# Strassen's method, one level, for the channel-mixing output product of batches 1 to 7

## The chip, the cores and the metric

The kernel runs on one core of one Trainium2 chip. The metric is the device time of one execution in microseconds (us). Before the change three runs gave 285.89, 285.95 and 286.25; their median, 285.95 us, is the time before. The engines are called PE (the matrix engine, TensorE), DVE (VectorE), ACT (ScalarE), POOL (GpSimd) and SP (SyncE, which here issues nearly all transfers).

## The reference

Attention over 8 batches, 8 heads, 576 positions and head dimension 64, with a plain window of 32 in heads 0 to 3 and a dilated one (every fourth position, reach 128) in heads 4 to 7, and a mixer behind it:

```python
attn = softmax(mask(q @ k.T / sqrt(D)))        # per batch and head
x    = (attn @ v) as [B, S, H * D]             # 8 x 576 x 512
h    = relu(x.T @ w_tok1) @ w_tok2             # token mixing, 576 -> 256 -> 576
u    = x + h.T
h2   = relu(u @ w_ch1) @ w_ch2                 # channel mixing, 512 -> 1536 -> 512
out  = u + h2
```

The change is in the last product, `relu(u @ w_ch1) @ w_ch2`, of 512 of the 576 positions of a batch (the last 64, the tail, are done for two batches together), and in the sum with u.

## The kernel before, in words

All operands of products are fp16, sums are fp32 in PSUM. A matmul takes a 128x128 block that stands still (lhsT) and streams up to 512 columns past it.

**One batch in the main line (`gen_main`, L747).** First the hidden layer: for each of 12 blocks `mb` of 128 hidden channels, four matmuls of 512 columns (L768, `gp`) and a ReLU into `gt` (L771; on ACT, of some blocks on DVE). In odd batches the tail of two batches comes in between (L759, `gt<-utt`). `gt` holds, for each hidden block, the columns of an even batch (0 to 511), of the tail (512 to 639) and of an odd batch (640 to 1151). Then the output product: for each of four row tiles `s` and each half of 256 output columns, 12 matmuls of 256 columns (L801, `yp`), so 96 per batch; in odd batches also 12 of 512 columns for the tail (L818), ahead of them. DVE adds u (L809) out of PSUM into `o32`, and SP stores two halves (L814). In the last batch the last row tile is cut into three narrower pieces (L787 to L795).

**Row order.** u's first two blocks of channels (plain heads) lie in natural row order. The other two (dilated heads) lie in the order of residue modulo 4: tile `s` holds rows s, s+4, s+8 and so on. That is why the second half of a row tile reads `gt` with a step of 4 (`a0:m0 + 512:4`, L804) and is stored with a stride. The hidden layer needs u with channels in the partitions: a DMA transpose (`uT_dma`, L682) turns all of u into `utm`, and ACT copies its dilated blocks into natural order into `utd` (`uT_place`, L690). Batch 0 and 1 do this on PE (`emit_uT`, L656).

**What is fed into the main line.** Each batch has a list of steps with a due time and a cost in us, written by hand (L1017 to L1064): values of the next batch (`values`, L592, heads 0 to 7), its token mixing (`emit_h1`, `emit_u` L630, `uT_dma`, `uT_place`), casts (L274), DMA transposes (`dma_steps`, L348) and placements (`place_steps`, L393) of q and k of the batch after next, its scores (`scores_twin`, L498), and loads three batches ahead. `interleave` (L827) advances a clock by the costs that the main line yields and emits a step when its due time has come. Each engine and each queue then works in the order of emission.

**Scores.** `scores_twin` runs for batches 2 to 7 in two groups, g = 0 (plain heads) and g = 1 (dilated heads): matmuls into six PSUM banks, exponentials on ACT (L534), and masks by multiplication on POOL (L112, `attp`, `attd`, `attt`).

**PSUM.** Eight banks: three called `main` in rotation (hidden layer, output product, one bank of scores), three `fl` (values, token mixing, u, scores), two `sc` (scores).

Of the kernel before, what the change touches and what calls it, by code (L numbers as in the profile page):

```python
# [9 lines left out]
FP16 = mybir.dt.float16  # L10
# [4 lines left out]
B = 8  # L15
# [53 lines left out]
def kernel(  # L69
# [19 lines left out]
    turn = {"main": 0, "sc": 0}  # L89

    def bank(tag, bufs, name, dtype=FP32):

        if tag in turn:
# [37 lines left out]
    qza = fixed("qz", [128, 4, 2, S])  # L131
    qz = [qza[:, i] for i in range(4)]
# [155 lines left out]
    xn, u16w, uT = {}, {}, {}  # L288
# [209 lines left out]
    def scores_twin(b, g):  # L498
# [72 lines left out]

        yield from small_exps(1)
        if b == 2:
            yield from small_exps(0)
        for hp in (2 * g, 2 * g + 1):
            for h in range(2):
                main(hp, h)
                if h and (g or b == 2):
                    mask(hp)
                    if b == 2 and hp % 2 == 0:  # L580
                        mask_tails()
                yield 0.0
        if b > 2:
            yield from small_exps(0)
            if g == 0:
                mask(0)
            mask_tails()
            if g == 0:
                mask(1)
# [66 lines left out]
    def emit_uT(b, cb):  # L656
        odd = b % 2
        p = bank("fl" if b or cb % 2 == 0 else "main", 3, f"tpu_{b}_{cb}", FP16)
        t = sb.tile([128, 640 if odd else 512], FP16, tag=f"ut{odd}", bufs=4, name=f"uT_{b}_{cb}")
# [22 lines left out]
    def uT_dma(b, tail):  # L682
# [3 lines left out]
        else:  # L686
            nc.sync.dma_start_transpose(out=uTm[i].rearrange("p x s t -> p (x s) t"),
                                        in_=u16w[b].rearrange("p x s c -> p (x s c)"))

# [57 lines left out]
    def gen_main(b):  # L747
# [28 lines left out]
        last = b == B - 1  # L776
        for s in ((4, 0, 1, 2, 3) if odd else (0, 1, 2, 3)):
            p = bank("main", 3, f"yp_{b}_{s}")
            o32 = sb.tile([128, DM], FP32, tag="o32", bufs=4, name=f"o32_{b}_{s}")
            if last and s == 3:  # L780
                for c0, n in ((0, 256), (256, 128), (384, 128)):
                    c = slice(c0, c0 + n)
                    if c0:
                        p = bank("main", 3, f"yq_{b}_{c0}")
                    a0 = m0 + (s if c0 else 128 * s)
                    for mb in range(NMB):
                        nc.tensor.matmul(  # L787
                            out=p[:, c], lhsT=gta[:, mb, a0:m0 + 512:4] if c0 else gta[:, mb, a0:a0 + 128],
                            rhs=w4[mb][:, c], start=(mb == 0), stop=(mb == NMB - 1))
                    nc.vector.tensor_tensor(out=blocks4(o32[:, c]), in0=blocks4(p[:, c]),  # L790
                                            in1=u16(b, s)[:, c0 // 128:(c0 + n) // 128], op=ALU.add)
                    nc.sync.dma_start(
                        out=out[b, 0:512, c].rearrange("(m r) c -> r m c", r=4)[s] if c0 else
                        out[b, 128 * s:128 * s + 128, c], in_=o32[:, c])
                    yield 0.65  # L795
            elif s < 4:
                for half in range(2):
                    c = slice(256 * half, 256 * half + 256)
                    for mb in range(NMB):
                        a0 = m0 + (s if half else 128 * s)  # L800
                        nc.tensor.matmul(  # L801
                            out=p[:, c],
                            lhsT=gta[:, mb, a0:m0 + 512:4] if half else
                            gta[:, mb, a0:a0 + 128],  # L804
                            rhs=w4[mb][:, c], start=(mb == 0), stop=(mb == NMB - 1))
                        if mb == 5:
                            yield 0.65
                    if half:
                        nc.vector.tensor_tensor(out=blocks4(o32), in0=blocks4(p), in1=u16(b, s), op=ALU.add)  # L809
                        for i in range(2):  # L810
                            d = slice(256 * i, 256 * i + 256)
# [283 lines left out]
```

## Time and profile before

| | |
|---|---|
| median of three runs | 285.95 us |
| the profiled execution's span | 284.4 us |
| PE busy | 276.2 us (97%) |
| DVE, ACT, POOL busy | 130.7, 136.9, 163.3 us |
| output product (L801), 744 matmuls of 256 columns | 85.8 us busy, mean 273 ns |
| hidden layer (L768), 144 + 144 + 96 matmuls of 512 columns | 54.7 + 54.6 + 25.8 us busy |
| DMA engines, mean busy share by the queues' packets | q1 69.2%, q0 7.9% |

How to read the profile: every line of a group gives source line, engine, operation, output <- input, shape and count, then busy time and the mean of one instruction in ns, then the idle time of the engine before these instructions and what ended it. In a timeline a row begins with the start and the length in us; several like instructions in a row are merged (x24), and idle time before a row stands in brackets with what ended it. Matmuls are pipelined: the next begins before the last has ended, so a matmul's own length says little of its pace. The profiled execution is one run; its span runs from the first to the last instruction.

### The profile page before, as it was taken

The page shows a single profiled execution, that of the slowest core. Times are in us where ns is not written, and L with a number is a line of the kernel's source. Part 1 is how long each engine was busy: PE and PEld are TensorE (multiplying, and loading weights), DVE is VectorE, ACT ScalarE, POOL GpSimd, SP SyncE. Part 2 cuts the span into 40 slices and gives each one's busy share as a digit, 9 for nine tenths or more (in the row PEclk, how much of TensorE's full clock was granted, in tenths as well). Part 3 has the DMA queues.
Part 4 walks back from the last instruction along what each step waited for, and adds up shares of the span by engine and source line. Part 5 has one row for each costly group of instructions (what it writes and reads, how often), then busy time and mean ns, then how long its engine had stood idle before and what let it go on. Part 6 is the DMA issues. An engine that isn't in the chain of part 4 may idle for free.

```text
span 284.4 us, 7021 instructions
## 1 busy us (share of the span) xinstructions
PE 276.2 (97%) x2850; PEld 210.9 (74%) x2850; DVE 130.7 (46%) x275; ACT 136.9 (48%) x270; POOL 163.3 (57%) x220
## 2 busy tenths in 40 slices
PE   6899999999999999999999999999999999999995
PEld 2786677887676976697776976797767966896595
DVE  7776676356764155415640254426441274421022
ACT  2863765454454615383446625482546534225500
POOL 7980760587936998459961999179953930000000
PEclk9999999999999999999999999999999999999999
DMA  7999999984999999999979988299974210431023
GB/s 218 265 227 253 271 218 211 323 206 117 342 187 142 292 275 236 145 223 334 195 151 227 312 239 169 58 236 313 203 146 85 94 56 2 92 112 39 0 76 111
DMA packets 105695, 52.63 MB, mean 185 GB/s; under 512 B 73888, under 2 KB 104608, under 8 KB 105664
## 3 DMA queue, kind: packets, MB, share of 16 engines
q1 hardware_dynamic: 101424, 47.07, 69.2%
q0 software_dynamic: 2640, 3.94, 7.9%
q10 hardware_dynamic: 1600, 1.18, 1.4%
q8 instruction: 22, 0.36, 0.6%
q14 instruction: 9, 0.07, 0.1%
HBM read 37.07 MB, written 9.44 MB: 163 GB/s over the span
## 4 chain that ended last, share of the span: by engine, by line
PE 79%; DMA 7%; POOL 6%; SPq 2%; DVE 2%; issue 1%; ACT 1%; POOLq 0%; ACTq 0%
PE gp L768 25%; PE yp L801 25%; PE h1p L627 4%; PE gt L759 4%; PE up L639 4%; PE yp L818 3%; PE sc L510 2%; DMA l_k<-in_k_dram 2%; DMA w1p<-in_moe_w_tok_dram 2%; DMA kr<-c_k 2%; DMA l_q<-in_q_dram 2%; POOL c_q L102 1%; PE av L603 1%; PE av L608 1%; PE h1p L625 1%
## 5 line engine op out<-in xcount | busy, mean ns | idle before, releaser
L801 PE MATMUL yp<-w,gt 128*128 128x256 f16 x744 | 85.8, 273 | 0.0
L801 PEld LDWEIGHTS <-gt 128*128 128x128 f16 x744 | 76.1, 106 | 6.4
L106 ACT ACTIVATE gt<-gp 128x512 f16<-128x512 f32 x71 | 42.4, 597 | 73.5 <-PE gp L768 73.2
L768 PE MATMUL gp<-utd,w 128*128 128x512 f16 x144 | 54.7, 380 | 0.0
L768 PE MATMUL gp<-utm,w 128*128 128x512 f16 x144 | 54.6, 379 | 0.0
L768 PEld LDWEIGHTS <-w 128*128 128x128 f16 x384 | 38.9, 114 | 19.7 <-issue 0.5
L809 DVE TENSOR_TENSOR o<-yp,u 128x512 f32<-128x512 f32 x31 | 21.4, 692 | 63.4 <-PE yp L801 63.4
L112 POOL TENSOR_TENSOR attp<-attp,const 128x1280 f16<-128x1280 f16 x12 | 31.4, 2616 | 24.4 <-ACT attp L534 24.3
L112 DVE TENSOR_TENSOR xn<-av,rec 128x320 f16<-128x320 f32 x64 | 31.5, 492 | 2.2
L112 POOL TENSOR_TENSOR attd<-attd,const 128x1024 f16<-128x1024 f16 x12 | 25.4, 2134 | 1.9 <-ACT attd L534 1.9
L768 PE MATMUL gp<-uT,w 128*128 128x512 f16 x96 | 25.8, 380 | 0.0
L108 DVE TENSOR_SCALAR gt<-gp 128x512 f16<-128x512 f32 x25 | 17.2, 688 | 13.7 <-PE gp L768 13.0
L645 DVE TENSOR_TENSOR u<-up,xn 128x512 f16<-128x512 f32 x26 | 17.9, 690 | 6.2 <-PE up L639 6.2
L534 ACT ACTIVATE attp<-sc 128x480 f16<-128x480 f32 (+1 forms) x36 | 16.1, 536 | 7.3 <-PE sc L510 6.2
L102 POOL CAST c_k<-l_k 128x512 f16<-128x512 f32 x29 | 17.7, 622 | 2.1 <-DMA l_k<-in_k_dram 2.0
L102 POOL CAST c_q<-l_q 128x512 f16<-128x512 f32 x26 | 16.7, 648 | 2.5 <-DMA l_q<-in_q_dram 1.8
L106 ACT ACTIVATE h<-h1p 128x256 f16<-128x256 f32 x31 | 11.9, 384 | 11.9 <-PE h1p L627 11.5
L616 DVE RECIPROCAL rec<-av 128x5 f32<-128x5 f32 x64 | 12.2, 191 | 9.8 <-PE av L613 9.6
L399 POOL COPY kt<-kr 128x512 f16<-128x512 f16 x10 | 10.8, 1078 | 9.9 <-DMA kr<-c_k 7.7
L697 ACT COPY utd<-utm 128x512 f16<-128x512 f16 x12 | 12.7, 1117 | 5.8 <-DMA utm<-u 5.8
L102 POOL CAST vv<-l_vn 128x256 f16<-128x256 f32 x32 | 11.9, 413 | 4.0 <-DMA l_vn<-in_v_dram 4.0
L112 POOL TENSOR_TENSOR attt<-attt,const 128x512 f16<-128x512 f16 x12 | 13.9, 1162 | 0.0
(149 smaller groups left out, 465.2 us busy)
## 6 DMA issues: line engine op xcount, KB each, us to landing
out_dram<-o SPq DMA_DIRECT2D x71, 128.0 KB, 3.2
l_q<-in_q_dram SPq DMA_DIRECT2D x15, 512.0 KB, 6.7
l_k<-in_k_dram SPq DMA_DIRECT2D x14, 512.0 KB, 7.1
l_vn<-in_v_dram SPq DMA_DIRECT2D x32, 128.0 KB, 6.4
l_vd<-in_v_dram SPq DMA_DIRECT2D x16, 256.0 KB, 4.5
w<-in_moe_w_ch_dram POOLq DMA_DIRECT2D x6, 512.0 KB, 7.6
lt<-in_q_dram SPq DMA_DIRECT2D x8, 128.0 KB, 3.9
l_vt<-in_v_dram SPq DMA_DIRECT2D x8, 128.0 KB, 4.1
```

The lines of the kernel that those rows point to most:

```text
L102: eng.tensor_copy(out=out, in_=in_)
L106: nc.scalar.activation(out=out, in_=in_, func=AF.Relu)
L108: eng.tensor_scalar_max(out=out, in0=in_, scalar1=0.0)
L112: eng.tensor_tensor(out=out, in0=x, in1=y, op=ALU.mult)
L534: nc.scalar.activation(out=out, in_=in_, func=AF.Exp, scale=0.125)
L616: nc.vector.reciprocal(out=rec[:, :, 0], in_=av[:, :, 64])
L627: nc.tensor.matmul(out=p, lhsT=w[:, s, j], rhs=x[:, s, c], start=False, stop=(s == 3))
L645: nc.vector.tensor_tensor(out=u16(b, s), in0=blocks4(p), in1=blocks4(xn[b][:, s]), op=ALU.add)
L697: nc.scalar.copy(out=natural(uTd[:, cb - 2]), in_=uTm[i][:, cb].rearrange("p r m -> p m r"))
L768: nc.tensor.matmul(out=p, lhsT=w3_block(cb, mb), rhs=uT[(b, cb)][0], start=(i == 0), stop=(i == 3))
L801: nc.tensor.matmul(out=p[:, c], lhsT=gta[:, mb, a0:m0 + 512:4] if half else gta[:, mb, a0:a0 + 128], rhs=w4[mb][:, c], start=(mb == 0), st ...
L809: nc.vector.tensor_tensor(out=blocks4(o32), in0=blocks4(p), in1=u16(b, s), op=ALU.add)
```

## The change

With the operand of 512 rows and 1536 hidden channels cut into A11, A12, A21, A22 (256 rows, 768 channels each) and `w_ch2` into B11, B12, B21, B22 (768 channels, 256 columns each), the output product of batches 1 to 7 is computed with seven products of 256 x 768 x 256 in place of eight (Winograd's form). Each is 12 matmuls of 256 columns.

- Sums of activations, on DVE, fp16 (`gate_sums`): A11 - A21 in place of A21, then A21 + A22 - A11 and A21 + A22 and A12 - (A21 + A22 - A11); three of them into the part of `gt` of the other parity or onto its columns. Each is made in two halves of three hidden blocks (128 x 768 elements): the first subtraction after blocks 3 and 6, the other three after blocks 9 and 11.
- Four sums of weights, once, in batch 0 (`weight_sum`, 128 x 1536 elements each), in the room of `qz` and of batch 0's transposed u.
- The output stage (`gen_out`): products X1, W1, X2, W2, X3, X4, W3. The X products accumulate in one `main` bank, which DVE reads between them (`with_u`, sum with u, four times); the W products go to another, read three times (`with_t`). The third `main` bank is `spare` and serves everything else meanwhile. Between X3 and X4 the main line asks for 0.9 us of other steps (`fill`); `interleave` gives it those due within 4 us. In odd batches the tail product comes first, in the last batch between X3 and X4.
- The rows of a product are in natural order for all columns, so u's dilated blocks are turned back into natural order by DMA transposes on SP (`u_natural`), from `utd`, and in batch 1 from its `uT` tiles. There are four stores of 256 x 256 per batch in place of eight.
- Scores: the second group is due later (9.5 to 9.8 us after the first in odd batches, 7.8 in even ones, 4.5 before), and in group 1 the remaining small exponentials come ahead of the main ones, and masks directly behind them.
- Batch 0 keeps the old product.

```diff
+        if tag == "main" and spare:
+            tag, bufs = f"main{spare[0] % 3}", 1
+        elif tag in turn:
...
+        early = b == 2 or g == 1
         yield from small_exps(1)
-        if b == 2:
+        if early:
             yield from small_exps(0)
...
+    def u_natural(b):
+        u = u16w[b]
+        if turned(b):
+            nc.sync.dma_start_transpose(out=u[:, 2:4].rearrange("p x s c -> p (x s) c"),
+                                        in_=uTd.rearrange("p x t -> p (x t)"))
+            return
+        for cb in (2, 3):
+            nc.sync.dma_start_transpose(out=u[:, cb], in_=uT[(b, cb)][0])
...
+    def weight_sum(i):
+        b11, b12 = w4a[:, 0:6, 0:256], w4a[:, 0:6, 256:512]
+        b21, b22 = w4a[:, 6:12, 0:256], w4a[:, 6:12, 256:512]
...
+        a, b = {1: (b12, b11), 2: (b22, wsum[1]), 3: (b22, b12), 4: (b21, wsum[2])}[i]
+        nc.vector.tensor_tensor(out=wsum[i], in0=a, in1=b, op=ALU.subtract)
+
+    def gate_sums(b, g, last):
...
+        s3, s2, s1 = gta[:, lo, r2], gta[:, lo, o0:o0 + 256], gta[:, lo, o0 + 256:o0 + 512]
...
+        if not last:
+            tt(s3, gta[:, lo, r1], s3, ALU.subtract)
+            return
+        tt(s2, gta[:, hi, r2], s3, ALU.subtract)
+        tt(s1, s2, gta[:, lo, r1], ALU.add)
+        tt(gta[:, hi, o0:o0 + 256], gta[:, hi, r1], s2, ALU.subtract)
...
+        def product(rows, k0, weights, first, parts):
+            for p, a, c in parts:
+                for mb in range(6):
+                    r = rows + 128 * a
+                    nc.tensor.matmul(out=p, lhsT=gta[:, k0 + mb, r:r + 128], rhs=weights[:, mb, c],
...
+                yield 0.0025 * (c.stop - c.start)
...
+        x, w = both(px), both(pw)
+        yield from product(m0, 0, w4a[:, 0:6, 0:256], True, x)
+        with_u(px, 0, 0)
+        yield from product(m0, 6, w4a[:, 6:12, 0:256], True, w)
+        with_t(0, 0, w)
+        store(0, 0)
+        yield from product(o0, 0, wsum[2], False, x)
+        with_u(px, 1, 0)
...
+        yield from product(m0 + 256, 0, wsum[3], True, w)
+        yield from product(o0 + 256, 0, wsum[1], False, x)
+        with_u(px, 1, 1)
+        with_t(1, 1, w)
+        store(1, 1)
+        if last:
+            yield from tails()
+        else:
+            yield ("fill", 0.9)
+        yield from product(o0, 6, w4a[:, 6:12, 256:512], False, x)
+        with_u(px, 0, 1)
+        store(0, 1)
+        for part in w if last else [None]:
+            yield from product(m0 + 256, 6, wsum[4], False, [part] if last else w)
+            with_t(1, 0, [part] if last else w)
+            store(1, 0, part)
...
+            if b and mb in (3, 6, 9, 11):
+                gate_sums(b, (mb // 3 - 1) % 2 if mb < 11 else 1, mb > 6)
...
+            steps += at(27.0, 1.5, [lambda i=i: weight_sum(i) for i in (1, 2, 3, 4)])
         elif b == 1:
+            steps += at(1.0, 0.0, [lambda: u_natural(1)])
...
-            steps += score_steps(3, 21.0, 4.6, lag=0.1)
+            steps += score_steps(3, 21.0, 9.5, lag=0.1)
...
+            steps += at(2.0, 0.0, [lambda b=b: u_natural(b)])
...
-                steps += at(2.0, 0.6, cast_steps(b + 2)) + score_steps(b + 2, 16.6 + 1.25 * late, 4.5)
+                steps += at(2.0, 0.6, cast_steps(b + 2)) + score_steps(b + 2, 16.6 + 1.4 * late, 9.8 if b % 2 else 7.8)
```

More of the change, by code (lines that the diff above doesn't have):

```diff
@@ L131 @@
     qza = fixed("qz", [128, 4, 2, S])
+    wsum = {}
     qz = [qza[:, i] for i in range(4)]
@@ L658, in emit_uT @@
         p = bank("fl" if b or cb % 2 == 0 else "main", 3, f"tpu_{b}_{cb}", FP16)
-        t = sb.tile([128, 640 if odd else 512], FP16, tag=f"ut{odd}", bufs=4, name=f"uT_{b}_{cb}")
+        if odd:
+            t = sb.tile([128, 640], FP16, tag="ut1", bufs=4, name=f"uT_{b}_{cb}")
+        else:
+            if b not in uT0:
+                uT0[b] = sb.tile([128, 4, 512], FP16, tag="ut0", bufs=1, name=f"uT_{b}")
+            t = uT0[b][:, cb]
         eng = nc.scalar if cb == 2 else nc.vector
@@ L775, in gen_main @@
                 yield 0.9
[L776 to L777 removed]
+            if b and mb in (3, 6, 9, 11):
+                gate_sums(b, (mb // 3 - 1) % 2 if mb < 11 else 1, mb > 6)
+        if b:
+            yield from gen_out(b)
+            return
+        for s in range(4):
             p = bank("main", 3, f"yp_{b}_{s}")
             o32 = sb.tile([128, DM], FP32, tag="o32", bufs=4, name=f"o32_{b}_{s}")
[L780 to L811, printed above, removed]
[L812 to L825 removed]
@@ new lines, in gen_main @@
+            for half in range(2):
+                c = slice(256 * half, 256 * half + 256)
+                for mb in range(NMB):
+                    a0 = s if half else 128 * s
+                    nc.tensor.matmul(
+                        out=p[:, c], lhsT=gta[:, mb, a0:512:4] if half else gta[:, mb, a0:a0 + 128],
+                        rhs=w4[mb][:, c], start=(mb == 0), stop=(mb == NMB - 1))
+                    if mb == 5:
+                        yield 0.65
+                if half:
+                    nc.vector.tensor_tensor(out=blocks4(o32), in0=blocks4(p), in1=u16(b, s), op=ALU.add)
+                    for i in range(2):
+                        d = slice(256 * i, 256 * i + 256)
+                        o = out[b, 0:512, d].rearrange("(m r) c -> r m c", r=4)[s] if i else \
+                            out[b, 128 * s:128 * s + 128, d]
+                        nc.sync.dma_start(out=o, in_=o32[:, d])
+                yield 0.65
@@ L837, in interleave @@
                 try:
-                    t += next(main)
+                    cost = next(main)
                 except StopIteration:
                     main = None
+                    continue
+                if not isinstance(cost, tuple):
+                    t += cost
+                    continue
+                need = cost[1]
+                while need > 0 and steps and steps[0][0] <= t + 4.0:
+                    _, cost, fn = steps.pop(0)
+                    fn()
+                    t += cost
+                    need -= cost
     def warm(n):
```

99 lines of the change are left out of this document (77 added, 22 removed).

## The prediction

> **What bounds the kernel now.** I read the page first, then the timeline of the last batch, then the timelines of PE, ACT, DVE, POOL and SP around the places that the change touches.
>
> ```profile
> span 284.4 us, 7021 instructions
> PE 276.2 (97%) x2850; PEld 210.9 (74%) x2850; DVE 130.7 (46%) x275; ACT 136.9 (48%) x270; POOL 163.3 (57%) x220
> PE   6899999999999999999999999999999999999995
> L801 PE MATMUL yp<-w,gt 128*128 128x256 f16 x744 | 85.8, 273 | 0.0
> ...
> L697 ACT COPY utd<-utm 128x512 f16<-128x512 f16 x12 | 12.7, 1117 | 5.8 <-DMA utm<-u 5.8
> ```
>
> PE is busy in every slice but the first two and the last, and its biggest group is the one the change rewrites. A busy PE in this profile is not yet a full one, since a matmul's own 273 ns overlap the next one's. The pace is in the timeline of the last batch:
>
> ```profile
> 270.68 8.02 PE L801 MATMUL yp<-w,gt 128*128 128x256 f16 x72
> 273.50 0.69 DVE L809 TENSOR_TENSOR o<-yp,u 128x512 f32<-128x512 f32 x1 [1.93 <-PE yp L801]
> ...
> 279.85 1.50 PE L787 MATMUL yq<-w,gt 128*128 128x128 f16 x24
> 280.05 0.42 DVE L790 TENSOR_TENSOR o<-yp,u 128x256 f32<-128x256 f32 x1 [0.62 <-PE yp L787]
> 280.50 1.54 SPq L792 DMA_DIRECT2D out_dram<-o  x3
> ...
> 281.39 0.29 DVE L790 TENSOR_TENSOR o<-yq,u 128x128 f32<-128x128 f32 x1 [0.38 <-PE yq L787]
> ```
>
> 72 matmuls take 8.02 us with the last one's 0.273 in it: (8.02 - 0.273) / 71 = 0.109 us each. Twelve take 1.31 us. The 24 of the first row tile end their issue at 270.68 + 24 x 0.109 = 273.30, and VectorE (DVE) starts on them at 273.50: a result can be read 0.2 us after PE has gone on. PE is thus the bound, and a matmul less is 0.109 us less as long as PE is never made to wait. That is what the rest is about.
>
> **What is removed.** Per batch 1 to 7, eight products of 12 matmuls become seven: 12 x 0.109 = 1.31 us, and over seven batches 9.17 us. The span would go from 284.4 to 275.2. The measured median, 285.95, is 1.5 us above the profiled span, and I take this offset as constant.
>
> **What is added on the path.** The seven products share two banks, X and W, in the order X1 W1 X2 W2 X3 (fill) X4 W3. Each X product accumulates onto the bank that DVE has just been asked to read, so X(n+1) starts only after that read. A read is complete 0.2 + 0.69 us after the product's last issue, and then PE has to see it:
>
> ```profile
> 58.13 0.69 DVE L385 COPY kt<-tp_k 128x512 f16<-128x512 f16 x1 [0.25 <-PE tp_k L378]
> ...
> 58.88 0.44 PE L510 MATMUL sc<-qt,kt 64*128 64x160 f16 x8 [0.47 <-DVE kt L385]
> ```
>
> DVE ends at 58.82, PE goes on at 58.88: about 0.05 more, so 0.94 us in all. Between X1 and X2 and between X2 and X3 stands a W product of 1.31 us, which hides it. Between X3 and X4 stands only the fill, which takes the second group of scores:
>
> ```profile
> 156.12 0.62 PE L510 MATMUL sc<-qt,kr 64*128 64x128 f16 x16
> 156.58 0.28 PE L510 MATMUL sc<-tt,kt 64*128 64x64 f16 x8
> 156.79 8.71 PE L801 MATMUL yp<-w,gt 128*128 128x256 f16 x78
> ```
>
> From 156.12 to 156.79 it covers 0.67 us, whatever the planner's 0.86 says. Batches 1 to 5 lose 0.27 each, **1.35**. Batch 6 has no scores left (nothing for batch 8) and loses the whole **0.94**; in batch 7 the tail's product of 2.6 us covers it.
>
> **The four sums over gt.** For each half of the blocks one subtraction runs early and three run last, the second half's after ReLU 11, and X2 reads their result. In batch 2 the output product and this ReLU lie so:
>
> ```profile
> 118.92 0.82 PE L801 MATMUL yp<-w,gt 128*128 128x256 f16 x6
> ...
> 119.12 0.60 ACT L106 ACTIVATE gt<-gp 128x512 f16<-128x512 f32 x1 [0.70 <-PE gp L768]
> ```
>
> The ReLU ends 0.8 us after the stage begins. No row shows DVE with two fp16 operands of SBUF. From above: 256 elements of fp32 take 0.42 and 512 take 0.69, so 768 at that rate take 0.96. From below: a contiguous fp16 copy of 512 takes
>
> ```profile
> 25.32 0.41 DVE L102 COPY uT<-tpu 128x512 f16<-128x512 f16 x1
> ```
>
> that is 0.28 less than fp32, half the cost per element over a fixed 0.15, so 768 take 0.55. I take 0.55, the row of the same type and layout. The last three then end at 0.85 + 1.65 = 2.5, the evacuation of X1 queued behind them at 3.19, and X2 could start at 3.24. It wants to start at 2.62 where nothing else lies between: batches 6 and 7 lose **0.6** each. In batches 2 and 4 the first scores (0.7) lie inside X1, in 1, 3 and 5 the tail's 2.6 us come first, and it is hidden.
>
> The early sums cost DVE about 8 x 0.55 = 4.4 us per batch, the three extra evacuations 2.1; DVE has room:
>
> ```profile
> 67.60:88.00 20.40, 20.40 (x221) 14.12 (x219) 14.81 (x31) 9.24 (x20) 14.04 (x17) 1.00 1.04 229
> ...
> 100.00:132.00 32.00, 31.86 (x323) 24.60 (x321) 13.86 (x29) 15.11 (x30) 23.76 (x29) 1.00 0.98 236
> ```
>
> (length, then busy us of PE, PEld, DVE, ACT, POOL, clock, DMA share, GB/s). It is tight only in batch 1, 14.8 of 20.4 us, where most ReLUs are its own. The three sums at block 9 stand ahead of two sums of u (s = 2 and 3) in DVE's queue; the scores that open the output stage reuse those sums' banks.
>
> ```profile
> 116.52 0.69 DVE L645 TENSOR_TENSOR u<-up,xn 128x512 f16<-128x512 f32 x1 [0.17 <-PE up L639]
> 117.39 0.69 DVE L645 TENSOR_TENSOR u<-up,xn 128x512 f16<-128x512 f32 x1 [0.18 <-PE up L639]
> 118.69 0.69 DVE L645 TENSOR_TENSOR u<-up,xn 128x512 f16<-128x512 f32 x1 [0.61 <-PE up L639]
> 119.67 0.95 PE L510 MATMUL sc<-qt,kt 64*128 64x160 f16 x14
> ```
>
> From 117.2, 1.65 us bring DVE to 118.9, the two sums of u end at 120.2, and the scores want the last of these banks at about 120.2. So it just fits, and any delay of DVE here becomes PE's: I put **0.4** on each of batches 2 and 4, with 0 and 1.5 as ends.
>
> These sums run while GpSimd (POOL) copies kt. The Trainium skill ("SBUF — State Buffer", SBUF: two separate sides) says that a VectorE instruction with two SBUF inputs and a GpSimd instruction reading SBUF exclude each other for their whole length. No row of before can show it, since every two-input DVE row above reads PSUM with one operand. By that page the 0.4 would go to its upper end and beyond, and it is weighed as the first rival.
>
> **Moved scores.** The second group of scores now runs 2.6 us before the batch's end. In batch 2 its six exponentials stand ahead of the copy of utd's second block in ACT's queue:
>
> ```profile
> 124.95 0.38 ACT L534 ACTIVATE attt<-sc 128x256 f16<-128x256 f32 x1 [0.94 <-PE sc L510]
> 125.23 2.06 ACT L534 ACTIVATE attd<-sc 128x512 f16<-128x512 f32 x4
> ...
> 127.41 2.13 ACT L697 COPY utd<-utm 128x512 f16<-128x512 f16 x2
> ```
>
> The exponentials hold ACT for 127.41 - 124.95 = 2.46, the copy takes 1.12. Counted from the stage's start, with 0.75 for the first scores (my estimate, between the 0.67 and the 0.95 of the rows above): the second scores end at 5 x 1.31 + 0.75 + 0.67 = 7.97, the exponentials at 10.6, the copy at 11.7. The next batch starts at 7.3 + 0.94 + 2.62 = 10.86 and reads that block after two matmuls and one head's values, 0.7 later: 11.56. **0.2** each for batches 2 and 4; in 3 and 5 the copies come before the scores. POOL's masks move too:
>
> ```profile
> 117.71 1.08 POOL L399 COPY kt<-kr 128x512 f16<-128x512 f16 x1 [5.18 <-DMA kr<-c_k]
> ...
> 130.13 4.21 POOL L112 TENSOR_TENSOR attd<-attd,const 128x1024 f16<-128x1024 f16 x2
> 134.30 1.16 POOL L112 TENSOR_TENSOR attt<-attt,const 128x512 f16<-128x512 f16 x1
> ...
> 146.42 1.07 POOL L399 COPY kt<-kr 128x512 f16<-128x512 f16 x1 [2.23 <-PE up L639]
> ```
>
> and batch 3 begins with
>
> ```profile
> 131.36 0.38 PE L768 MATMUL gp<-utd,w 128*128 128x512 f16 x1
> ```
>
> The second group's masks need 135.46 - 130.13 = 5.3 us and ended 4.1 us into batch 3. The first group still holds POOL until 130.13 - 118.92 = 11.2 after the stage's start, so they end at 16.5, 5.6 us into a batch that begins at 10.86: 1.5 later than before. Head 6, the first to need the last of them, is due at 6.1 us; before the placements POOL idled 2.23 and 5.18 us in these two batches, which takes the 1.5. Hidden; 0.5 us less slack would show at head 6.
>
> **u turned back.** Batch 1 sends two transposes of 512 columns, the others one of 1024, through SP. They wait for nothing late and their readers come 20 us after. But what stands behind them on SP is late in batch 1:
>
> ```profile
> 71.64 4.89 SPq L207 DMA_DIRECT2D l_vn<-in_v_dram  x4
> 77.12 1.31 SPq L351 DMA_TRANSPOSE tt<-c_t  x1
> 80.58 0.64 SPq L207 DMA_DIRECT2D l_vt<-in_v_dram  x1
> ...
> 85.05 0.61 POOL L102 CAST vv<-l_vt 64x512 f16<-64x512 f32 x1 [3.24 <-DMA l_vt<-in_v_dram]
> 85.61 1.07 POOL L399 COPY kt<-kr 128x512 f16<-128x512 f16 x1
> ...
> 86.97 1.07 POOL L399 COPY kt<-kr 128x512 f16<-128x512 f16 x1
> ...
> 88.61 0.65 PE L510 MATMUL sc<-qt,kt 64*128 64x160 f16 x14
> ```
>
> Two at 1.31 are 2.6 us, of which the gap between 76.53 and 77.12 takes 0.6: l_vt comes 2.0 later, POOL waits for it in order, and the placement that ended at 88.04 ends at 90.04, while its scores want it at 88.8. PE waits **1.2** (0 if SP catches up, 2.6 if nothing absorbs it). In the later batches the loads lead by a batch and four fewer stores leave room on SP: nothing.
>
> **Small ones.** Four sums of weights in batch 0, about 0.95 each (1536 elements at the same rates; 1.75 at most), stand near the copy of kt for which PE waits 0.47 already: **0.3** (0 to 1). At the end the stores of two blocks queue on SP where three small ones did (1.54 us for three): **0.6** later.
>
> **Sum.** 1.35 + 0.94 + 1.2 (batches 6, 7) + 0.8 + 0.4 + 1.2 + 0.3 + 0.6 = 6.8 lost of 9.17; 2.4 us remain. 285.95 - 2.4 = **283.6 us**.
>
> **The rivals.**
> 1. *DVE and POOL shut each other out* (slower). Place: the three sums at block 9. If each waits for one of POOL's 1.07 us copies, 3.2 us come ahead of the sums of u, of which none is slack. Batches 1, 2 and 4 lose some 3 each, 9 us, less the 0.8 counted: 283.6 + 8.2 = 291.8 at worst, and at half of it 287.7. It decides from 0.8 us per batch in three batches on. For it: POOL is busy 23.8 of 32 us. Against: the three are short and back to back, and POOL's copies end soon after. This is the lock of the Trainium skill's page cited above.
> 2. *DVE's sums run at the fp32 rate*, 0.96: X2 waits 1.2 more in batches 6 and 7 and about 1 more in 2 and 4: 283.6 + 4.4 = 288.0. Against it stands the fp16 row.
> 3. *SP and DMA become late*: DMA's share is about 1.0 from batch 1 to 3. If the added turns (1.25 to 1.3 us of issue each) pass fully on in batches 1 to 3, 2.6 + 1.3 + 1.3 against the counted 1.2: 283.6 + 4.0 = 287.6; a third to half of it, 285 to 285.6, is likelier.
> 4. *All uncertain waits are hidden*: without 0.8, 0.4, 1.2, 0.3 and half of 0.6 the loss is 3.8: 280.6.
>
> That the product isn't shortened I leave out: 84 for 96 matmuls stand in the code.
>
> **How the numbers follow.** Forecast (282 to 285) 50%, rival 4 20%, rival 3 13%, rival 1 9%, rival 2 8%. The range, 280.4 to 287.2, holds the forecast, most of rivals 4 and 3 and the mild end of 1. A difference under 0.2%, 0.57 us, can't be told from none here. Faster: the first two and a part of the third, 0.73; same 0.09; slower 0.18.
>
> **What would show it.** Right: 84 matmuls per batch at 0.109; PE waiting some 0.27 at X4 for DVE in batches 1 to 5 and 0.9 in batch 6; DVE's sums at 0.55; the first scores of batch 1 near 90. Wrong: sums at 0.9 or more, or stretched where POOL is busy; PE idle at the scores that open batches 2 and 4; idle of ACT or DMA origin at a batch's start.

## The result, and the profile after

The change makes the kernel slower: 299.81 us (median of 4 runs, 294.27 to 301.25) against 286.1 (285.89 to 286.72) on the same chip, a ratio of 1.035, 95% interval 1.0275 to 1.0433. The prediction was 283.6 with a range to 287.2. The changed kernel's own runs lie further apart than those of the kernel before: the ratios here and below come from the runs within 1.5% of a kernel's fastest, here 294.27 and 298.56, whose mean, 296.4, is the figure used further on, while the profile is of the run of 301.05.

The page after, with the rows that answer to those shown of before:

```profile
span 299.1 us, 6936 instructions
PE 274.7 (92%) x2766; PEld 201.3 (67%) x2766; DVE 191.0 (64%) x358; ACT 137.2 (46%) x270; POOL 171.7 (57%) x220
PE   6999999899996899999998999999298999989994
PEclk9999999999997999999999999999789999999999
...
L727 DVE TENSOR_TENSOR gt<-gt 128x768 f16<-128x768 f16 x56 | 45.2, 827 | 8.3 <-ACT gt L109 7.4
...
L772 PE MATMUL yx<-w,gt 128*128 128x256 f16 x168 | 20.9, 272 | 3.7 <-DVE o L749 2.3
```

PE has 84 matmuls less, as it should, but it isn't busy in every slice any more: at slice 13 there is a dent, at slice 29 a hole. Three slices are also short of clock (13, 29 and 30). DVE has gone from 130.7 to 191.0 us, of which the sums are 45.2. The view of one line gives their spread (ns: least, median, most):

```profile
L727 DVE TENSOR_TENSOR gt<-gt x56: 541/559/6375, 75.7 to 284.5; 128x768 f16<-128x768 f16 x56
```

The median is the 0.55 us of the prediction. One sum takes 6.4 us. The timeline around it, DVE, POOL and PE:

```profile
208.17 6.38 DVE L727 TENSOR_TENSOR gt<-gt 128x768 f16<-128x768 f16 x1
214.46 0.18 DVE L619 RECIPROCAL rec<-av 128x5 f32<-128x5 f32 x1
214.68 0.49 DVE L115 TENSOR_TENSOR xn<-av,rec 128x320 f16<-128x320 f32 x1
...
207.85 0.63 POOL L105 CAST c_k<-l_k 128x512 f16<-128x512 f32 x1
208.41 0.63 POOL L105 CAST c_q<-l_q 128x512 f16<-128x512 f32 x1
...
213.71 0.42 POOL L105 CAST vt<-l_vx 128x256 f16<-128x256 f32 x1
...
215.23 0.40 PE L628 MATMUL h1p<-xn,w1t 128*128 128x256 f16 x1 [5.28 <-DVE xn L115]
```

The casts follow each other every 0.56 us and last 0.63, so each starts before the one ahead has ended. Thirteen of them overlap the sum, twelve of which start after it. The last ends at 214.13, and 0.4 us later the sum is through. The sum is issued and counted as busy, but for most of that time it stands still. Behind it in DVE's queue stands the last piece of xn, and PE waits 5.28 us for that. In batch 1 three sums together take 4.62 us beside placements, and the scores wait:

```profile
87.42 4.62 DVE L727 TENSOR_TENSOR gt<-gt 128x768 f16<-128x768 f16 x3
...
93.29 0.89 PE L514 MATMUL sc<-qt,kt 64*128 64x160 f16 x7 [2.83 <-DVE u L648]
```

PE's waits that bear on the change, by what ended them (us in total, times, longest):

```profile
PE h1p L628 <- DVE xn L115: 6.4, 3, 5.3
PE sc L514 <- DVE u L648: 3.5, 4, 2.8
...
PE yx L772 <- DVE o L749: 2.3, 3, 0.8
PE yx L772 <- DVE o L787: 1.5, 3, 0.8
PE sc L514 <- DVE kt L389: 1.0, 1, 1.0
...
PE gp L912 <- ACT utd L841: 0.3, 2, 0.2
```

Behind the two longest waits TensorE runs at half clock, in the windows view for 3.4 and 6.8 us (length, busy us of PE, PEld, DVE, ACT, POOL, then clock, DMA share, GB/s):

```profile
93.06:96.46 3.40, 3.12 (x22) 1.45 (x22) 2.27 (x5) 1.87 (x5) 0.00 (x0) 0.50 0.72 43
212.50:219.30 6.80, 4.07 (x17) 2.36 (x18) 3.23 (x4) 0.78 (x3) 3.35 (x7) 0.50 1.09 154
```

A busy microsecond there does about half the work (four matmuls of L630 take 1.06 us from 215.42 on and 0.60 from 207.87 on), so a stall costs more than its length. The Trainium skill ("TensorE: Matmul & The Clock Gate", Part 1) has the clock fall to half after an idle window of about 3.4 us and rise after as long a busy one; the two lengths here, 3.4 and twice 3.4, fit it. But the clock fell 2.6 us after the last matmul ahead of the first wait (90.46 to 93.06) and 2.5 us after the one ahead of the second (209.95 to 212.50), so here less than 3.4 us of idle time was enough.

### The profile page after: what moved, and what is told of

Same layout as the page of the kernel before. It is cut to its first block, busy times and chain, and to the rows that moved or that the text cites. A ratio compares the mean times of both kernels' runs of the same rounds, so it can differ in the third digit from the quotient of the medians.

```text
span 299.1 us, 6936 instructions
## 1 busy us (share of the span) xinstructions
PE 274.7 (92%) x2766; PEld 201.3 (67%) x2766; DVE 191.0 (64%) x358; ACT 137.2 (46%) x270; POOL 171.7 (57%) x220
## 5 line engine op out<-in xcount | busy, mean ns | idle before, releaser
L772 PEld LDWEIGHTS <-gt 128*128 128x128 f16 x600 | 57.6, 98 | 13.7 <-issue 5.2
L727 DVE TENSOR_TENSOR gt<-gt 128x768 f16<-128x768 f16 x56 | 45.2, 827 | 8.3 <-ACT gt L109 7.4
L787 DVE TENSOR_TENSOR o<-yx,u 128x512 f32<-128x512 f32 x28 | 19.3, 690 | 28.4 <-PE yx L772 28.4
L772 PE MATMUL yx<-w,gt 128*128 128x256 f16 x168 | 20.9, 272 | 3.7 <-DVE o L749 2.3
L772 PE MATMUL yx<-wsum_a,gt 128*128 128x256 f16 x168 | 20.6, 272 | 0.7 <-DVE o L787 0.7
L105 POOL CAST c_q<-l_q 128x512 f16<-128x512 f32 x26 | 17.7, 684 | 3.1 <-DMA l_q<-in_q_dram 2.4
L105 POOL CAST c_k<-l_k 128x512 f16<-128x512 f32 x29 | 18.4, 643 | 1.5 <-DMA l_k<-in_k_dram 1.5
L538 ACT ACTIVATE attt<-sc 128x256 f16<-128x256 f32 x24 | 8.9, 396 | 21.0 <-PE sc L514 17.6
L794 DVE TENSOR_TENSOR o<-yw,o 128x512 f32<-128x512 f32 x19 | 13.1, 692 | 6.9 <-PE yw L772 6.4
L657 DVE TENSOR_TENSOR u16t<-up,xn 64x512 f16<-64x512 f32 x7 | 4.8, 689 | 19.5 <-PE up L653 19.5
```

What stands on the lines that cost most here:

```text
L105: eng.tensor_copy(out=out, in_=in_)
L538: nc.scalar.activation(out=out, in_=in_, func=AF.Exp, scale=0.125)
L727: nc.vector.tensor_tensor(out=out, in0=a, in1=b, op=op)
L772: nc.tensor.matmul(out=p, lhsT=gta[:, k0 + mb, r:r + 128], rhs=weights[:, mb, c], start=(first and not mb and (not a or len(parts) > 2)), ...
L787: nc.vector.tensor_tensor(out=grid(o[(i, j)]), in0=grid(p), in1=u, op=ALU.add)
L794: nc.vector.tensor_tensor(out=t, in0=p, in1=t, op=ALU.add)
```

## The experiments

Theory A: a sum with two inputs in SBUF is shut out while POOL works, and what stands behind it on DVE makes PE wait. Theory B: SP's queue and DMA, with u's turn back, are late. Theory C: DVE simply has too much to do at these places. The medians of the kernel before, measured beside each run, lay between 286.5 and 287.0. A `...` in an edit stands for lines left out.

### Which part costs

**No gate sums.** The products take what lies in the places of the sums.

```diff
-            if b and mb in (3, 6, 9, 11):
-                gate_sums(b, (mb // 3 - 1) % 2 if mb < 11 else 1, mb > 6)
```

> The changed kernel without the sums over gt (its products read what stands in gt, so the output is not the reference's). Theory A, VectorE's two-operand sums and GpSimd exclude each other and the delayed VectorE queue stops PE: all idle of PE behind VectorE's u and xn rows goes, and the time is 285.95 - 9.17 + 1.35 (X4) + 1.0 (batch 6) + 3.4 (X1 behind the tail's bank in batches 1, 3, 5) + 0.7 + 0.6 + 0.6 = about 284.4 us. Theory B, SP and DMA are late because of u's turning back: the time stays above 292. Theory C, the output stage with two banks is itself too slow: above 288.

287.8 us (285.4 to 290.3), ratio 1.004 (1.001 to 1.007). 8.6 of the changed kernel's 296.4 hang on the sums. It is 3.4 above what theory A had here. Two waits that the kernel before doesn't have stand high in the list of PE's waits:

```profile
PE yx L772 <- DVE o L749: 2.3, 3, 0.8
PE sc L514 <- POOL kt L403: 2.0, 2, 1.0
```

**The first of them mended as well.** In batches 1, 3 and 5 the products' first bank is the one that the tails' product has just filled: the scores take a bank while the tails' product is under way, before the bank to be spared is noted down.

```diff
-            yield next(tail)
+            first = next(tail)
             spare.append(turn["main"] + 1)
             turn["main"] += 1
+            yield first
```

> The same, still without the sums over gt (output not the reference's), and in odd batches the first scores get the spare bank, so that X1 no longer gets the bank of the tail. Theory A with the bank: 3.4 us less than without this edit, about 281.0 us, and no gap of 1.1 us ahead of X1 in batches 1, 3 and 5. If that gap was only waiting that would have come later anyway: less than 1 us of difference.

285.5 us (283.6 to 286.8), 0.9955 (0.993 to 0.998). The row of L749 is gone and 2.3 us with it. The other wait stays, at 120.8 and 122.2 in batch 2:

```profile
PE sc L514 <- POOL kt L403: 2.1, 2, 1.1
```

and behind it the windows view has the clock at half again:

```profile
123.30:126.60 3.30, 3.30 (x18) 2.27 (x16) 0.94 (x2) 3.30 (x9) 0.75 (x1) 0.50 0.86 184
```

**No turn back of u.** With the sums in place, u's dilated half is left unturned.

> The changed kernel without turning u's dilated half back (u is then added in the other row order, the output is not the reference's). Theory A: still 293 to 301 us, the sums as long as in the changed kernel. Theory B: 5 us or more below the changed kernel.

296.9 us (292.5 to 303.1), 1.0215 (1.017 to 1.026): within the changed kernel's own spread, and by the ratios some 4 us under it where theory B asked for 5 or more. So theory B isn't borne out as the main cause, though a part isn't excluded. In this profile the scores of batch 1 still wait 3.12 us for u, but the sum of batch 5 that took 6.38 us takes 0.72: that hold isn't always there, and whether the edit or the run decides isn't shown. The same without sums and with the bank mended:

> The kernel without sums and with the tails' bank kept apart (285.5), now also without the transposing DMA that turns u's dilated half back (leaves out that turn as well as the sums, so two parts of u and the gate's sums aren't as the reference has them). Theory B (that DMA stands on SP ahead of the transposes that GpSimd's placements of batch 2 wait for): the wait of the scores of batch 2 for kt (1.35 and 1.15) and the half clock behind it go, 282 to 283.5. If the placements are late for another reason, the wait stays and the time is 285 to 286.

284.3 us (281.6 to 290.5), 0.988 (0.982 to 0.994). The wait for kt in batch 2 is gone from the list and the profiled span is 281.6 against 283.6, but the intervals of the two runs overlap. So rival 3 seems real in kind: one late set of placements, in batch 2 and not in batch 1, and some 2 us.

### What it is about the sums

**The same sums in the kernel before.** Eight per batch at the same places, written to a scratch tile that nobody reads.

```diff
...
+            if b and mb in (3, 6, 9, 11):
+                idle_sums(b, (mb // 3 - 1) % 2 if mb < 11 else 1, mb > 6)
```

> The kernel before with the eight sums per batch of 128x768 fp16 on VectorE added at the same places, written to a scratch tile that nobody reads. Theory A: sums stretched to several us where GpSimd works without a pause, PE stopped behind VectorE, and 4 to 12 us above the kernel before. Theories B and C (the sums are harmless): within 1.5 us of the kernel before, sums at 0.55 us each.

315.2 us (313.4 to 322.1), 1.097 (1.092 to 1.103): 28.7 us, more than twice the upper end expected. The row of 28 of these sums (ns: least, median, most):

```profile
L755 DVE TENSOR_TENSOR scr<-gt x28: 541/557/7956, 74.6 to 298.5; 128x768 f16<-128x768 f16 x28
```

PE's longest wait in the list of waits:

```profile
PE h1p L625 <- DVE xn L112: 19.1, 4, 7.5
```

No product was changed here, so neither SP, nor banks, nor the order of the products is needed for the loss.

**Unread sums with one input in PSUM**, in the kernel before at the same places: longer each, so more work for DVE.

```diff
...
+            nc.vector.tensor_tensor(out=scr, in0=p, in1=gta[:, mb - 1, c], op=ALU.subtract)
...
```

> The kernel before, with eight sums per batch whose results nobody reads, at the same places as in the earlier run that added unread sums (which took 315.2), but with one input in PSUM: 128x512 at about 0.69, so 5.5 us of VectorE per batch where those needed 4.4. Theory A (the two inputs in SBUF are what lets GpSimd shut them out): 287 to 291, no sum over 0.75. Theory C (any work on VectorE at these places delays xn and u): 310 or more, as with the sums from SBUF.

295.9 us (295.4 to 298.0), 1.033 (1.030 to 1.036). 56 instructions, none stretched:

```profile
L752 DVE TENSOR_TENSOR scr<-gp,gt x56: 673/691/693, 74.9 to 279.8; 128x512 f16<-128x512 f32 x56
```

and in the list of PE's waits

```profile
PE gp L775 <- DVE scr L752: 6.0, 5, 1.7
```

With 5.5 us of DVE per batch it costs 9 us where 4.4 us from SBUF cost 28.7. The 9 weren't expected: 6.0 of them are PE waiting for the block's bank, which these sums hold. So theory A stands, and C has a part.

**Stand-ins in the changed kernel.** Each gate sum becomes a maximum over 128x480 of the gate: same places, same blocks waited for, one input (`SN` is 160, of three blocks each).

```diff
...
+        def standin(blocks, rows):
+            nc.vector.reduce_max(out=seen[:, 0:1], in_=gta[:, blocks, rows.start:rows.start + SN],
+                                 axis=mybir.AxisListType.XY)
...
-            tt(s3, gta[:, lo, r1], s3, ALU.subtract)
...
+            standin(lo, r1)
...
```

> The changed kernel with a stand-in of the same length in the place of each gate sum: a maximum over 128x480 of the gate into one column, one input, no second one in SBUF (an estimate of 0.55 us; the traces show none, so its own row decides), waiting for the same blocks. Leaves the gate's sums out, so the products take what lies there. Theory A (being shut out is the cost): no stand-in over 0.7 us, no wait of 5 us and no half clock in batch 5, 288 to 290.5, within 3 us of the kernel without sums (287.8). Theory C (VectorE's queue is simply too full at these places): 294 or more, near the changed kernel. Between the two, both, in that proportion.

291.4 us (290.8 to 292.9), 1.018 (1.015 to 1.020).

```profile
L729 DVE TENSOR_REDUCE seen<-gt x56: 635/655/657, 76.5 to 274.5; 128x1 f16<-128x480 f16 x56
```

This splits the 8.6: from 296.4 to 291.4 is what being shut out costs, 5.0; from 291.4 to 287.8 is DVE's queue, 3.6, at stand-ins that last 0.1 longer than a free sum. The 5.0 shares the changed kernel's spread: it is 8.4 by the median of all its runs (299.8), and by the interval of its ratio it is uncertain by some 2 us.

**Pauses on POOL**: a memset of one column behind every cast and placement of batches 3 to 7.

> The changed kernel with a memset of 128x1 on GpSimd behind every cast and every placement for batches 3 to 7 (nothing else moved). Theory A in its sharper form (the sum isn't shut out by GpSimd being busy, but by instructions that follow each other with no gap, each starting before the last has ended): the memsets, which read nothing, open a gap, no sum is over 1.5 us in batches 2 to 5, and the time falls to 288 to 292. If a sum must wait until GpSimd's whole queue is empty, the longest sum stays at 5 us or more and the time at 294 or above, for the queue is now longer.

295.2 us (294.6 to 298.2), 1.031 (1.025 to 1.037), not to be told from the changed kernel. The worst sum took 2.86 and, in batches 2 to 5, 2.09 us, so the sharper form of theory A isn't borne out by the time; whether it is the missing gap that lets POOL keep DVE out for 13 casts stays open.

### Where the sums stand

**Late sums.** Batches 1 to 5 have their first sums after block 10, the other six after block 11, when POOL's casts and placements are mostly done.

```diff
...
+            if 0 < b < 6 and mb == 10:
+                for g in range(2):
+                    gate_sums(b, g, 3)
+            if 0 < b < 6 and mb == 11:
+                for i in (2, 1, 4):
+                    for g in range(2):
+                        gate_sums(b, g, i)
...
```

> The changed kernel with the same eight sums per batch, of batches 1 to 5 all after blocks 10 and 11 of the gate instead of after 3, 6, 9 and 11; so late GpSimd has done its casts and placements (in batch 5 of the changed kernel they end at 222.3, block 10 is evacuated at 227.3). Theory A (a sum is shut out for as long as GpSimd works without a pause, and h1 and the scores wait behind it): nearly every sum at 0.55, no half clock in batch 5, 287 to 290 us, near the kernel without sums (287.8) plus some 1 us for X2 that now waits. Theory C (the 56 sums' own 31 us on VectorE are the cost, wherever they stand): no better than 294.

293.1 us (290.3 to 300.6), 1.019 (1.012 to 1.025), between the figures of theories A and C. The profile is of the run of 300.6: no gate sum took over 1.65 us, but one of the four sums of weights in batch 0 was shut out by casts and masks, and PE waited 5.8 us behind it:

```profile
62.75 8.53 DVE L718 TENSOR_TENSOR wsum_b<-w,wsum_a 128x1536 f16<-128x1536 f16 x1
```

and in the list of PE's waits

```profile
PE tp_q L382 <- DVE uT L105: 5.8, 1, 5.8
```

**Late sums, a mended bank and another order of the products** (X1 W1 X2 W2 X3 W3 X4: no product goes on in a bank that has just been read), with s1 and s4 behind the second product.

```diff
...
+        for i in (1, 4):
+            for g in range(2):
+                if b < 6 or g:
+                    gate_sums(b, g, i)
...
```

> All seven products and all sums. Sums of batches 1 to 5 late, as in the run with late sums, but only s2 ahead of the products, s1 and s4 behind the second; the tails' bank kept apart; in batches 1 to 6 the order X1 W1 X2 W2 X3 W3 X4, so that no product waits for the evacuation of the bank it goes on in. Theory A: the sums at 0.55, 3 x 1.13 (bank), 5 x 0.27 and 1.02 (X4), 0.6 (X2 of batch 6) gone: 283 to 286, ahead of the kernel before by 0 to 1%. Theory C: 290 or more.

320.8 us (320.4 to 322.8), 1.120 (1.115 to 1.126): the worst kernel of all, and the miss is telling. There POOL starts its masks. In batch 2:

```profile
130.96 7.72 DVE L727 TENSOR_TENSOR gt<-gt 128x768 f16<-128x768 f16 x4
131.31 2.65 POOL L115 TENSOR_TENSOR attp<-attp,const 128x1280 f16<-128x1280 f16 x1 [3.45 <-ACT attp L538]
...
139.33 2.72 PE L775 MATMUL yx<-wsum_a,gt 128*128 128x256 f16 x12 [6.40 <-DVE o L790]
```

and over all batches, in the list of PE's waits,

```profile
PE yx L775 <- DVE o L790: 26.0, 5, 6.4
```

Four sums of 0.55 take 7.7 us beside the masks, and X3 waits for the evacuation queued behind them, 26.0 us in five batches; its own 2.72 us, where twelve matmuls take 1.47 at full clock, show the half clock behind the wait. Four of the eight sums, moved by some 2 us (from 128.74, where s2 ends, to 130.96), make the kernel 27.7 us slower than the last one, though two waits are mended.

**Sums after blocks 9, 10 and 11, all ahead of the products** (batches 1 to 5), with the bank, the order, the weight sums moved to a rest of POOL (t = 22.0 in place of 27.0 and on) and u's turn back of batches 2 to 5 behind the transposes (12.5 in place of 2.0).

> All seven products and all sums, everything placed by what the traces so far showed. Of batches 1 to 5 the first sums stand after block 9 and three each after blocks 10 and 11, ahead of the products and so ahead of GpSimd's masks; the four sums of weights at once where VectorE and GpSimd both rested (47.8 to 51.8 in the kernel without sums); the tails' bank kept apart; X1 W1 X2 W2 X3 W3 X4 in batches 1 to 6; u's turn back of batches 2 to 5 behind the transposes of q and k. Theory A: the sums at 0.55 to 1, no half clock, 283 to 286, faster than the kernel before or level. Theory C (the sums' own time on VectorE): 290 or more.

295.6 us (292.2 to 297.9), 1.027 (1.022 to 1.032). Most sums are at 0.55 here (the longest takes 3.66), and still theory C's figure came out: they stand ahead of u's additions, and the scores' banks come free behind those.

```profile
PE sc L514 <- DVE u L648: 8.2, 5, 2.3
```

**Sums formed out of PSUM**, with the same mends: 24 instructions of 128x256 per batch, maximum with 0 and then plus or minus the other piece; all ReLUs of batches 1 to 7 go to ACT.

```diff
...
+            nc.vector.scalar_tensor_tensor(out=out, in0=a, scalar=0.0, in1=c, op0=ALU.max, op1=op)
...
```

> The same as the run before it in the list, but no gate sum has two inputs in SBUF: each is formed out of a block's bank in PSUM (maximum with 0, then plus or minus the other piece), 24 instructions of 128x256 per batch at some 0.41 (a sum of 128x256 out of PSUM took 406 ns), 9.7 us of VectorE per batch in place of 4.4 and of two evacuations of 0.69 that go to ScalarE. The 26 sums of u, which read PSUM, took 671 to 693 ns with GpSimd at work, so these shouldn't be stretched wherever they stand. Theory A (what costs is being shut out, not the work): 282 to 287, with no instruction of these over 0.45. Theory C: slower than the run before it, 290 or more, since VectorE has 4 us per batch more to do.

292.8 us (292.6 to 294.6), 1.023 (1.020 to 1.025): theory C's figure, 5.8 over the upper end of theory A's. Yet none is stretched:

```profile
L728 DVE SCALAR_TENSOR_TENSOR gt<-gp,gt x168: 412/415/426, 70.4 to 278.2; 128x256 f16<-128x256 f32 x168
```

and in the view by line (busy us and mean ns, then DVE's idle time ahead of them and what ended it):

```profile
L728 DVE SCALAR_TENSOR_TENSOR gt<-gp,gt 128x256 f16<-128x256 f32 x168 | 62.8, 419 | 28.4 <-ACT gt L109 21.7 <-PE av L616 4.3 <-PE sc L514 0.9
```

DVE stands idle ahead of them, 21.7 us for ACT, with everything else queued behind. So the hold can be avoided by the form of the instruction, at the price of a fuller queue.

### Until it is faster

Theory D: lock and place in DVE's queue together are the whole cost of the sums. Each kernel after the first of these moves what the trace of an earlier one showed to be held or late.

**Late sums with all mends** (first sums after block 10, six after block 11; bank, order, weight sums, u's turn).

> All products and all sums. The kernel with late sums (first sums after block 10, the other six after block 11), and with the other mends of the earlier one of that kind: the four sums of weights together in the rest of VectorE and GpSimd, the tails' bank kept apart, X1 W1 X2 W2 X3 W3 X4, u's turn back of batches 2 to 5 behind the transposes. Against that one the sums don't stand ahead of u's additions, for which the scores' banks waited 1.96 three times, 2.55 and 0.78. Theory D (lock and place in VectorE's queue together are the whole cost): 284 to 287.5, level with the kernel before. If it stays at 290 or more, something is at work that no run has named yet.

289.5 us (287.9 to 291.4), 1.010 (1.007 to 1.014), 2.0 over the range forecast; one sum of batch 1 held 3.48 us.

**Batch 1 all after block 11, and steps pulled ahead behind X3 as in the changed kernel** (`yield ("fill", 0.9)`).

> All products and all sums: the last kernel with late sums and all mends (289.5) with two more. In batch 1 the two first sums stand after block 11 instead of 10, where one was held 3.48 us by placements, the scores behind it waited 2.93 and half a clock of 3.4 us followed (some 4.6 us together); and steps are again pulled ahead in the place behind X3, as in the changed kernel (the tokens' copy then isn't 1.12 late twice but 0.33). Theory D (lock and place in VectorE's queue are the whole cost): 283 to 285.5, under the kernel before by 0.4 to 1%. Otherwise 288 or more.

290.2 us (288.6 to 294.5), 1.010 (1.006 to 1.014). A miss: batch 1's last sum now ran into the mask, and one wait took the other's place.

```profile
88.65 7.85 DVE L727 TENSOR_TENSOR gt<-gt 128x768 f16<-128x768 f16 x8
...
93.07 3.02 POOL L115 TENSOR_TENSOR attp<-attp,const 128x1280 f16<-128x1280 f16 x1 [1.25 <-ACT attp L538]
...
97.16 2.08 PE L775 MATMUL yw<-w,gt 128*128 128x256 f16 x9 [3.97 <-DVE o L751]
```

**With the two s4 sums behind the first product's evacuation.**

> The run before it in the list with the two s4 sums behind the first product's evacuation instead of ahead of it, so that X2 doesn't wait 1.1, 1.18, 0.66 and 0.56 for that evacuation. Theory D: 0.5 to 3 us under the run before it. If GpSimd's masks (128.29 in batch 2 of the last kernel) start before these sums are through, they are held for 2.6 us each and it is 1 to 5 us slower.

294.9 us (293.4 to 296.6), 1.029 (1.025 to 1.033). In batches 2 and 4 it did what it should (X2 came 1.1 us late before, X2 and W2 together come 0.3 late now); in 3 and 5 the masks were there first. PE's waits, the second of them the one of batch 1 as before:

```profile
PE yw L775 <- DVE o L797: 4.8, 2, 2.4
PE yw L775 <- DVE o L751: 3.6, 1, 3.6
```

**Batch 1's sums after blocks 6, 9 and 11** (and s4 back ahead of the products).

> All products and all sums: the last kernel with late sums, mends and pulled steps (290.2, profiled span 287.8), with the sums of batch 1 at other places: the two first after block 6 (about 80.5, GpSimd at rest from 80.3 to 82.1), three after block 9 (about 84.5, at rest from 83.8 to 86.2), three after block 11 (from 89, between placements and the masks that start at 93.1). Theory D: the wait of 4.21 behind the sum held in the mask and the half clock of 6.8 us behind it go, the other batches stay as they were: 283 to 285.5, 0.4 to 1% under the kernel before. If a sum of batch 1 is held there too, 287 or more.

289.2 us (288.8 to 290.8), 1.009 (1.007 to 1.012). Missed again: the sum after block 9 started 0.25 us after a cast had started and took 4.28 us.

**The same with s4 behind the evacuation in batches 2, 4, 6 and 7 only.**

> The run before it in the list, with the s4 sums of batches 2, 4, 6 and 7 behind the first product's evacuation (in the earlier run that had them there in all batches, X2's wait of 1.14 fell to 0.31 in batches 2 and 4, while in 3 and 5 they ran into the masks and cost 2.63 each; here 1, 3 and 5 keep them ahead). Theory D: 1 to 2.5 us under the run before it, 281.5 to 284.

285.9 us (284.4 to 287.9, 12 runs), 0.9972 (0.995 to 0.9995): 0.3% ahead of the kernel before, at the edge of what can be told, and 1.9 over the range forecast. Batch 1's three sums after block 9 still took 4.38:

```profile
86.25 4.38 DVE L727 TENSOR_TENSOR gt<-gt 128x768 f16<-128x768 f16 x3
```

**Those three after block 8**, nothing else.

```diff
-            if b in (1, 6, 7) and mb in (9, 11):
-                gate_sums(b, mb // 2 - 4, *((2, 1, 4) if mb < 11 or b == 1 else (2, 1)))
+            if b in (6, 7) and mb == 9 or b == 1 and mb == 8 or b in (1, 6, 7) and mb == 11:
+                gate_sums(b, int(mb == 11), *((2, 1, 4) if mb < 11 or b == 1 else (2, 1)))
```

> The fastest kernel so far (285.9, profiled span 282.6) with one step moved: the three sums of batch 1 that stood after block 9 (the first was held 3.32 us from 87.3 by a cast and placements; the scores behind it waited 1.59, 0.97 and 0.55 and the clock was at half for 3.4 us) stand after block 8, about 83, where GpSimd works with pauses or rests until 86.2. Theory D: those waits go or fall to some 1 us, 282 to 284.5, about 1% under the kernel before. If a sum of batch 1 is held in the casts from 82 to 83.8, or those after block 11 are held longer, no better than 285.

282.4 us (281.5 to 287.1), 0.986 (0.982 to 0.991): 1.4% under the kernel before and 14 us under the changed one, with all seven products and all sums. Its page:

```profile
span 280.3 us, 6949 instructions
PE 268.3 (96%) x2766; PEld 199.1 (71%) x2766; DVE 181.3 (65%) x358; ACT 137.2 (49%) x270; POOL 165.3 (59%) x220
```

DVE's sums of batch 1 in its timeline:

```profile
82.53 1.79 DVE L727 TENSOR_TENSOR gt<-gt 128x768 f16<-128x768 f16 x3
88.83 4.21 DVE L727 TENSOR_TENSOR gt<-gt 128x768 f16<-128x768 f16 x3 [0.34 <-ACT gt L109]
```

PE's waits for DVE's kt and for its sums of u:

```profile
PE sc L514 <- DVE kt L389: 0.5, 1, 0.5
PE sc L514 <- DVE u L648: 0.4, 1, 0.4
```

The three sums moved now take 1.79. Three others of batch 1 still take 4.21, but what stands behind them is the tails' evacuation, which PE needs only for W1, behind the rest of the tails' product and X1:

```profile
93.70 1.47 PE L775 MATMUL yw<-w,gt 128*128 128x256 f16 x12 [0.22 <-DVE o L751]
```

In the kernel with batch 1 all after block 11 the same wait was 3.97. So what a held sum costs is what waits behind it. The one step moved here gave 3.5 us. No kernel without sums was run with all these mends, so what the sums still cost in this one isn't known, and theory D's "whole cost" isn't shown.

## Why the prediction was wrong

The step that failed is the one put as "it just fits": the delay of DVE was counted only at block 9 of batches 2 and 4, at 0.4 each with 1.5 as the upper end, and the early sums were passed as "DVE has room". Room is a share over 20 or 30 us; what PE waited for was one instruction, shut out, at the head of the queue: in the profiled run PE's waits for xn and u come to 9.9 us, and without the sums the kernel takes 8.6 less.

- **9.17 us saved.** Right as far as the matmuls go: 2850 became 2766, and twelve take 1.47 us, as 11 x 0.109 + 0.272 has it.
- **X4, 0.27 and 0.94.** Right to the digit. In batch 1 X3's last issue is at 103.33 + 12 x 0.109 = 104.64 and X4 starts 0.95 later (0.67 of it under the scores); in batch 6 it is 265.75 + 2 x 0.109 = 265.97 and 266.91.

```profile
103.33 1.47 PE L772 MATMUL yx<-wsum_a,gt 128*128 128x256 f16 x12
...
105.59 1.47 PE L772 MATMUL yx<-w,gt 128*128 128x256 f16 x12
...
265.75 0.38 PE L772 MATMUL yx<-wsum_a,gt 128*128 128x256 f16 x2
266.91 1.47 PE L772 MATMUL yx<-w,gt 128*128 128x256 f16 x12 [0.78 <-DVE o L787]
```

- **X2 in batches 6 and 7, 0.6; utd 0.4 in all.** Right: with L787's 0.78 of batch 6's X4 taken off its 1.5, 0.7 of idle is left for the two; with the 0.16 by which each time the last matmul's 0.273 outlasts the pace of 0.109, that is 1.0 to 1.1 against 1.2. The row of utd has 0.3.
- **A sum takes 0.55.** Right where nothing holds it (541 to 559 ns): rival 2 was wrong.
- **u's additions late by 0.8 in two batches.** Right for these (3.5 less the 2.8 of batch 1 leaves 0.7) and wrong in where it looked. The worst sums were in batch 1 beside placements (2.83 of wait) and in batch 5, an early sum at block 3, beside casts (5.28), where what waited was xn and h1 and not u. Neither place was walked through.
- **SP, 1.2 in batch 1.** Wrong place: it shows only once the sums are gone, in batch 2, as 2.0 to 2.1 us of wait and half a clock for 3.4 us. The first scores of batch 1 do start near 90 (90.01), the sign that was named, but no wait stands ahead of them.
- **Weights, 0.3.** The wait for kt went from 0.47 to 1.0, so 0.5 in the profiled run, but 5.8 in the run where one was shut out.
- **Not seen: the tails' bank**, 2.3 us. The code alone would have shown it.
- **Half clock after a stall.** Not in any term, though the row of the clock was read: it was full until the end, since the longest wait in the kernel before, behind its first matmuls, is 0.7 us.
- **Rival 1 was the main cause**, with too small a price (291.8 at worst) and too small a chance (9%). It took for granted that a sum waits for one of POOL's instructions, 1.07 us at most; it waited for up to 13 in a row. And "POOL is busy 23.8 of 32 us" was in the quoted rows.

From 283.6 to 296.4 are 12.8 us. The sums cost 8.6 where 2.0 was counted (X2 1.2, u 0.8), which is 6.6. The other 6.2 stand in the kernel without sums: the bank 2.3; the placements of batch 2 some 3.7 (2.0 of wait, half of 3.4 of clock) where 1.2 was counted, 2.5. That leaves 1.4, less than the spread of the changed kernel's runs. About half of it is lost ahead of batch 1, whose hidden layer begins at 68.44 there and at 67.47 in the kernel before, where 0.3 was counted for the weights; the rest is unassigned. How the 8.6 divide is shown by the stand-ins (5.0 shut out, 3.6 queue, with the spread said there). That place counts is shown by the last step, which moved three sums and nothing else and gave 3.5 us; the last kernel as a whole also has the bank, the order, the weights and u's turn mended, so its 14 us aren't the place's alone.

## What to carry to other kernels

When a change gives VectorE an instruction with two inputs in SBUF, lay GpSimd's timeline beside it at every place where it runs, and price it at the length of the whole string of GpSimd instructions that it can meet, not at one. Put it where GpSimd waits for somebody, or where what is queued behind it isn't needed soon, or give it one input in PSUM, if the queue has room for it. And count a stall of PE twice: waits of 2.8 and 5.3 us here cost the wait and then 3.4 and 6.8 us at half clock.

## What the runs showed of the hardware

- A two-input sum that needs 0.55 us took 6.38 us beside 13 casts, one in the kernel before 7.96, and a weight sum of 0.95 took 8.53. The Trainium skill ("SBUF — State Buffer", SBUF: two separate sides) has the first to start hold the shared ports for its whole instruction while the other blocks. The traces agree, and add that the blocked one needn't get its turn at the next instruction's end. At other times it does: the first sum of the changed kernel (75.74, 2.19 us) came through as the mask beside it ended (77.51), and the next cast, started at 77.46, took 0.94 in place of 0.63. What decides isn't settled.
- The maxima with one input, and the sums with one input in PSUM, were never held: 635 to 657 ns (56 maxima), 673 to 693 (56 sums), 412 to 426 (168 fused sums), in kernels where POOL was busy 56 to 57% of the span.
- In the kernel without sums and with the bank mended, the clock went to half behind two waits of 1.1 and 1.0 us close together (120.8 and 122.2), with no idle stretch of 3.4 us: from 119.9 to 123.3 PE was busy for 1.51 us.
